# The order of 576 tasks, and the engine of 21 of them, in a fused attention and gated-MLP kernel on one core

## The chip, the core and the metric

The kernel runs on one core of one Trainium2 chip. Times are device microseconds (us) of one execution; the time of a kernel is the median of its runs. The core has five engines with a queue each: PE (matrix multiply), DVE (vector), ACT (activation functions), POOL (general, without access to PSUM) and SP, which only issues DMAs here. An engine works through its queue in program order and waits at an instruction until what it needs has been signalled.

## What is computed

A block with two branches over 2048 tokens of width 512. A vector `c` gives six modulation rows. Branch A is linear attention with 32 heads of 16 features, whose feature map is a pair of softmaxes; branch B is a gated MLP with 1376 hidden units. Inputs are bfloat16.

```
mod = silu(c) @ w_mod -> sa, ca, ga, sb, cb, gb
h = layernorm(x) * (1 + ca) + sa
q, k, v = split(h @ wqkv);  pq, pk = q @ w_phi, k @ w_phi        # per head
phi_q = [softmax(pq), softmax(-pq)];  phi_k = [softmax(pk), softmax(-pk)]
kv = sum over s of phi_k v;  z = sum over s of phi_k
o = (phi_q kv) / (phi_q z + 1e-6)
x = x + ga * (o @ wo)
h = layernorm(x) * (1 + cb) + sb
x = x + gb * ((sigmoid(h @ w_gate) * (h @ w_up)) @ w_down)
```

## The kernel before

The tokens are 16 tiles of 128. `w_phi` is folded into the weights of queries and keys, so one product gives `pk` directly. All work is cut into 1230 named tasks. Each task knows what it reads and writes and which engines may run it; one string, `ORDER`, lists all names, and that list alone decides the order. A name may carry the engine: `@A` for ACT, `@D` for DVE, `@P` for POOL; without it the first engine that the task allows is taken. `arrange` walks the list, checks that whatever a task needs stands ahead of it, and hands out buffers (8 PSUM banks, 7 feature buffers and so on) in the order in which the list sets them free; `emit` then issues the instructions:

```
for word in text.split():
    name, _, e = word.partition("@")
    t = self.tasks[name]
    t.eng = LETTER[e] if e else next(iter(t.alts))
    ...
    for b in t.bufs:
        if b.slot is None:
            b.slot = slots[b.cls].pop(0)
```

So each engine's queue is the list, cut down to the tasks of that engine. The lists of costs in the tasks are used by nothing in this program.

The names, by stage, with the lines of the profile (`t` is a tile, `g` a group of one or two tiles, `j` a quarter of the width):

- **Start.** `ld_*` are the loads on SP. `tpw` (PE) transposes the key weights, `wTc` (ACT, L664) copies them out of PSUM, `fold` (PE) multiplies them with `w_phi`, `foldc` (ACT, L685) copies the result. `st1_t` (DVE, L702/L703), `rs1_g`, `nmr1_g` and `xn1_t` (L727 on ACT, L731 on POOL) are the first normalization; `tph` (PE) or `xT1` (DMA) transposes it, `hm1_gj` (L751 on ACT, L753 on DVE or POOL) applies the modulation, which comes from `modc1` (PE) and `modc1c`.
- **Key pass**, for each tile: `K` and `V` (PE, L817 and L821), `e` (ACT, L776: two exponentials), `n` (DVE, L780: the sums), `r` (the reciprocal: L798 on DVE, L794 and L795 on ACT), `phi` (L787 on POOL or DVE), `va` (ACT, L836) and `kv` (PE, L282), which adds up in two PSUM banks for all 16 tiles. Features of tiles 11 and 13 to 15 go in four or two parts (`r14.4` is the part of tile 14 from group 4 on).
- **Hand-over.** `kvz0`, `kvn0`, `kvz1`, `kvn1` (DVE, L299 and L294) read the two banks when the last `kv` of each half is in.
- **Query pass**, for each tile: `Q`, `qe`, `qn`, `qphi` (L784), `pT` (a DMA that transposes), then `num` (PE, L326), `rd` and `u` (DVE), `oT`, `out` (PE, L356, with `wo` scaled by `ga` in `wo0` to `wo3` on POOL, L851), `x1`, `st2`, `rs2`, `xn2`. Queries of the first tiles run ahead, between the keys.
- **MLP**, in chunks of 1, 1, 2, 4, 4 and 4 tiles: `mod` (modulation), `gK.f` and `uK.f` (PE, L447: gate and up products of chunk K), `tg` (ACT), `hm` (DVE), `y` (PE, L485), `fin` and the store. `wd0` to `wd10` (POOL, L860) scale `w_down`.

The stages overlap as the list mixes them; nothing in the program waits for a whole stage.

Of the kernel before, what the change touches and what calls it, by code (L numbers as in the profile page):

```python
# [39 lines left out]
bd wdz warm0 c1 warm1_0 warm1_1 warm1_2 warm1_3 warm1_4 warm1_5 ld_x0b ld_x0a ld_wk0 tpw1 tpw0 warm1_6 warm1_7 c2 mask4 st1_3 st1_2 st1_1 ld_x1b rs1_2 rs1_1  # L40
nmr1_2 ld_wk1 xn1_3@A c3 wTc1 ld_x1a pmem tpw2 wTc0 nmr1_1 st1_6 wTc2 ld_wm00b st1_0 tpw3 xn1_1 tph13 tph10 xn1_2 tph22 tph20 tph21 wTc3 fold10 rs1_0@P fold12
st1_7 foldc10 ld_wm00a foldc12 fold11 modc1.0 rs1_4@P ld_x2b warm1_8 warm1_9 foldc11 modc1c0 st1_5 tph11 tph12 warm1_10 ld_wm01b warm1_11 st1_4 rs1_3@P
hm1_20@A xn1_0 nmr1_4 hm1_10 hm1_11@A hm1_21@A tph01 tph23 fold13 tph00 xn1_6 xn1_7 ld_wm01a st1_11 hm1_01@A foldc13 st1_10 modc1.1 K3a modc1c1@D ld_x2a
hm1_00@A tph02 nmr1_3 hm1_23 rs1_6@P hm1_13@A hm1_02 st1_9 st1_8 xn1_5 tph03 K0a tph41 hm1_03@A K2a tph40 xn1_4 hm1_22@A hm1_12@A hm1_41@A hm1_40 wqT1 nmr1_6
ld_x3a st1_15 fold01 K2b foldc01 tph42 hm1_42@A K0b K3b e0.0 ld_wv0 tph32 tph30 tph31 wqT3 tph33 rs1_5@P nmr1_5 K1a hm1_32 xn1_11 hm1_30@A st1_14 n0.0 st1_12
xn1_10 e2.0 xn1_9 K1b e3.0 rs1_8@P V3a V3b va3 V0a wqT2 xn1_8 V2a hm1_31@A V2b tph43 nmr1_8 xn1_15 xn1_14 ld_wmga wqT0 V0b fold03 V1a modca.0 modca.1 hm1_33
tph50 e1.0 n2.0 V1b K5a r0.0@A modcac hm1_50 n3.0 hm1_43@A foldc03 xT1_11 fold02 tph52 fold00 foldc02 phi0.0 va2 foldc00 xT1_10 va1 n1.0 va0 K5b K4a r3.0
st1_13 tph53 hm1_63@P hm1_60@P K4b hm1_62@P Q0 hm1_53@A tph51 Q1 ld_wmm2 r2.0@A tph82 hm1_51@A Q2 r1.0 phi3.0@D phi1.0@D qe0.0 Q4 hm1_82@A modc2.0 phi2.0@D
rs1_7@P nmr1_7 xn1_12 hm1_52 qe2.0 ld_wo xn1_13 kv0.0 kv1.0 kv2.0 tph83 kv3.0 qe1.0 qn0.0 qphi0.1@P xT1_12 e5.0 modc2.1 xT1_13 modc2c K6a K6b qphi0.0@P pT0
e4.0 qn2.0 tph80 qn1.0 hm1_80@A qphi2.1 qphi2.0 K7a K7b qe4.0 n4.0 V6 va6 r4.0@A n5.0 V5 va5 tph81 V4 qn4.0 phi4.0@D qphi1.1@P pT2 r5.0@A va4 qphi1.0@P  # L50
hm1_70@P K9 K8 hm1_61@P qphi4.0@P kv4.0 pT1 phi5.0 hm1_72@P qphi4.1 e6.0 hm1_83 hm1_81 V9 n6.0 V7 pT4 hm1_71 e9.0 va9 e7.0 va7 K11 n9.0 e8.0 e11.6 r6.0 r9.0@A
# [4 lines left out]
qn6.0 wo0 wo3 kv15.0 kvz0 kvn0 kv13.4 kv14.4 kv15.4 kvz1 kvn1 num0a num1a num2a wo2 rd0a wo_all rd1a qe3.0 u0a num0b num4a num1b rd0b Q11 qe5.0 rd2a u0b u2a
rd4a num2b qn3.0 u1a rd1b tpo0 Q8 qphi6.0@P qphi6.1@P oT0 out0 num4b rd2b u1b wd0 qe11.0 u2b qphi3.1@P qphi3.0@P x1_0 rd4b st2_0 qe8.0 Q7 qe7.0 tpo1 oT1 Q10
Q9 out1 Q15 oT2 rs2_0 qn5.0 nmr2_0 xn2_0 u4a u4b x1_1 qn7.0 tsw xnT0 out2 qphi5.1@P qphi5.0@P pT6 mod02 mod00 qphi7.0@P pT3 mod03@A mod01@A qe15.0 qphi7.1@P
Q13 g0.8 x1_2 tg0.8 g0.1 st2_1 wd1 rs2_1 tg0.1 u0.8 u0.1 g0.0 num3b g0.4 hm0.1 hm0.8 pT5 qe9.0 tg0.4 g0.9 wd2 u0.4 u0.9 rd3b u3b tg0.9 g0.5 num3a hm0.4 hm0.9
u0.2 u0.0 num6a tg0.5 tg0.0 rd3a u3a u0.5 g0.2 hm0.0 hm0.5 rd6a nmr2_1 qe10.0 tg0.2 oT4 g0.10 u0.10 wd6 hm0.2 g0.3 pT7 tg0.3 u6a g0.6 num6b u0.3 y0.0 y0.1  # L60
rd6b tg0.10 hm0.10 hm0.3 num5a num5b u6b rd5b wd3 wd4 wd5 oT3 oT6 xn2_1 qe13.0 tg0.6 rd5a y0.2 u5b g0.7 tg0.7 out4 u5a oT5 qn11.0 u0.6 u0.7 xnT1 num7a hm0.6
hm0.7 mod13@A mod12@A rd7a x1_4 y0.3 out3 qphi11.1@P qphi11.0@P x1_3 st2_3 out6 mod10@A mod11@A g1.2 tg1.2 g1.1 tg1.1 num7b wd7 u1.3 u1.2 hm1.2 u7a g1.4 u1.1
y0.4 rd7b hm1.1 u1.4 y0.5 tg1.4 hm1.4 g1.0 g1.10 u1.10 g1.3 u7b st2_2 rs2_2 tg1.10 tg1.3 hm1.10 hm1.3 pT11 out5 tg1.0 u1.7 g1.7 x1_6 nmr2_2 u1.0 hm1.0 g1.5
u1.5 x1_5 qn10.0 wd8 y0.6 g1.6 oT7 xn2_2 xn2_3 g1.8 y0.7 Q14 y0.8 wd10 tg1.7 tg1.5 hm1.5 out7 u1.8 u1.6 st2_4 tg1.6 xnT2 xnT3 wd9 x1_7 qphi10.0 Q12 hm1.7
st2_6 mod21@P mod20@P qphi10.1@P y1.0 pT10 tg1.8 mod22@A mod23@A hm1.6 g1.9 y1.1 y1.2 tg1.9 u1.9 y0.9 y1.3 y1.4 g2.5 y0.10 g2.6 st2_5 qe12.0 st2_7 hm1.8 qn9.0
tg2.5 qe14.0 rs2_4 hm1.9 rs2_3 nmr2_4 y1.5 u2.0 g2.1 g2.0 tg2.0 xn2_7@D hm2.0 nmr2_3 fin0 y1.6 g2.2 tg2.2 u2.6 u2.2 hm2.2 u2.1 num11b y1.7 g2.4 rd11b u11b
xn2_6@P xnT7 xnT6 u2.5 tg2.1 xn2_5 qphi9.1@P hm2.1 tg2.6 u2.8 xn2_4 hm2.5 g2.3 num11a rd11a u11a u2.9 qphi9.0@P xnT5 y1.8 xnT4 tg2.4 u2.4 hm2.4 hm2.6 tg2.3
g2.9 u2.3 hm2.3 g2.8 tg2.8 tg2.9 u2.7 mod41@P mod43@P mod32@P mod42@P mod31@P qn13.0 g2.10 hm2.8 g2.7 y1.9 num10a qn8.0 num10b y2.0 y1.10 tg2.7 hm2.7 rd10a
hm2.9 qphi8.0@P u2.10 pT9 y2.1 y2.2 y2.3 y2.4 y2.5 qn14.0 num9b rd9b qphi13.0 qphi8.1@P mod30@A mod33@A tg2.10 mod40@A y2.6 y2.7 g3.3 wr qphi13.1@P tg3.3 oT11
g3.0 u10a rd10b u10b pT8 oT10 hm2.10 qn15.0 g3.8 num9a rd9a u9a u3.0 out11 y2.8 g3.1 y2.9 qphi14.1 fin1 x1_11 u9b u3.3 hm3.3 st1 tg3.8 tg3.0 u3.8 num8a st2_11  # L70
num8b rd8b rd8a u8a pT13 qphi15.0 hm3.8 u8b u3.9 g3.4 u3.2 out10 x1_10 qphi14.0 oT8 oT9 hm3.0 st2_10 y2.10 g3.6 u3.6 qn12.0 rs2_6 out8 tg3.4 tg3.6 x1_8 hm3.6
# [987 lines left out]
```

## Time and profile before

| what | us |
|---|---|
| time before, median of 3 runs | 203.33 (203.19 to 203.52) |
| profiled execution, first to last instruction | 202.2 |
| DVE busy, whole span | 160.6 (79%) |
| ACT busy, whole span | 105.3 (52%) |
| POOL busy, whole span | 104.2 (52%) |
| first `num` of the query pass starts | 57.38 |
| first gate product of the second chunk starts | 77.5 |

The profiled execution has no time of its own beyond its span. The runs lie 1.0 to 1.3 us above that span, which is what lies around the first and the last instruction. The granted TensorE clock is 1.00 in every window up to 190 us and 0.97 behind it. All times within the execution are counted from its first instruction.

### The profile page before, as it was taken

The page shows a single profiled execution, that of the slowest core. Times are in us where ns is not written, and L with a number is a line of the kernel's source. Part 1 is how long each engine was busy: PE and PEld are TensorE (multiplying, and loading weights), DVE is VectorE, ACT ScalarE, POOL GpSimd, SP SyncE. Part 2 cuts the span into 40 slices and gives each one's busy share as a digit, 9 for nine tenths or more (in the row PEclk, how much of TensorE's full clock was granted, in tenths as well). Part 3 has the DMA queues.
Part 4 walks back from the last instruction along what each step waited for, and adds up shares of the span by engine and source line. Part 5 has one row for each costly group of instructions (what it writes and reads, how often), then busy time and mean ns, then how long its engine had stood idle before and what let it go on. Part 6 is the DMA issues. An engine that isn't in the chain of part 4 may idle for free.

```text
span 202.2 us, 4128 instructions
## 1 busy us (share of the span) xinstructions
PE 194.4 (96%) x1447; PEld 106.2 (53%) x1471; DVE 160.6 (79%) x376; ACT 105.3 (52%) x250; POOL 104.2 (52%) x146
## 2 busy tenths in 40 slices
...
DVE  3999999999999999998897796885969753326622
ACT  2899999999978975576531215212113420334100
POOL 3889978799699998867570066130030431000000
...
GB/s 169 329 262 239 289 232 111 114 71 261 396 254 77 133 109 51 82 39 108 117 79 80 53 79 85 100 104 52 26 26 81 2 78 54 28 5 26 28 54 57
DMA packets 49452, 22.92 MB, mean 113 GB/s; under 512 B 38065, under 2 KB 47634, under 8 KB 49426
## 3 DMA queue, kind: packets, MB, share of 16 engines
...
HBM read 11.58 MB, written 2.10 MB: 68 GB/s over the span
## 4 chain that ended last, share of the span: by engine, by line
PE 70%; ACT 15%; DVE 8%; issue 2%; POOL 2%; DMA 1%; POOLq 0%; DVEq 0%
PE y_ps L485 19%; PE u_ps L447 18%; PE g_ps L447 18%; PE a_ps L356 5%; ACT h1T L751 3%; ACT e L776 3%; ACT qe L776 2%; PE num L326 2%; PE k_ps L817 2%; DVE qks L780 2%; ACT wqk_f L685 2%; PE v_ps L821 2%; DVE ks L780 1%; DMA x_sb<-in_A_x_dram 1%; DVE phi L787 1%
## 5 line engine op out<-in xcount | busy, mean ns | idle before, releaser
L457 ACT ACTIVATE tg<-g_ps 128x512 bf16<-128x512 f32 (+5 forms) x66 | 28.7, 455 | 66.8 <-PE g_ps L447 39.9
L468 DVE SCALAR_TENSOR_TENSOR wmod_sb<-tg,u_ps 128x512 bf16<-128x512 bf16 (+4 forms) x63 | 30.2, 491 | 18.0 <-ACT tg L457 11.5
L485 PE MATMUL y_ps<-wd_sb,wmod_sb 128*128 128x512 bf16 (+4 forms) x180 | 44.2, 366 | 0.2
L447 PEld LDWEIGHTS <-wg_sb 128*128 128x128 bf16 (+1 forms) x252 | 21.9, 99 | 16.1 <-issue 0.2
L447 PEld LDWEIGHTS <-wu_sb 128*128 128x128 bf16 (+1 forms) x252 | 21.7, 99 | 15.9 <-issue 0.3
L784 POOL TENSOR_TENSOR qphi<-qe,qks 128x512 bf16<-128x512 bf16 x24 | 25.1, 1064 | 4.1 <-DMA pT<-qphi 1.4
L485 PEld LDWEIGHTS <-wmod_sb 128*128 128x128 bf16 (+1 forms) x187 | 17.1, 98 | 16.0 <-issue 0.6
L447 PE MATMUL u_ps<-wT_sb,wu_sb 128*128 128x512 bf16 (+2 forms) x124 | 23.8, 322 | 0.1
L447 PE MATMUL g_ps<-wT_sb,wg_sb 128*128 128x512 bf16 (+2 forms) x122 | 23.0, 321 | 0.2
L447 PE MATMUL g_ps<-wqk_sb,wg_sb 128*128 128x128 bf16 (+4 forms) x127 | 19.9, 287 | 0.1
L447 PE MATMUL u_ps<-wqk_sb,wu_sb 128*128 128x128 bf16 (+4 forms) x127 | 19.8, 286 | 0.2
L780 DVE TENSOR_REDUCE ks<-e 128x64 f32<-128x1024 bf16 (+2 forms) x22 | 19.3, 904 | 0.2
L492 DVE TENSOR_TENSOR ot<-y_ps,x 128x512 bf16<-128x512 f32 (+2 forms) x17 | 11.1, 654 | 10.1 <-PE y_ps L485 10.1
L780 DVE TENSOR_REDUCE qks<-qe 128x64 bf16<-128x1024 bf16 x16 | 19.1, 1204 | 0.0
L376 POOL TENSOR_SCALAR ve<-mv 128x2 f32<-128x2 f32 (+1 forms) x8 | 1.8, 226 | 33.4 <-DVE mv L366 33.3
L776 ACT ACTIVATE e<-k_ps 128x512 bf16<-128x512 f32 (+2 forms) x44 | 18.3, 536 | 0.0
L776 ACT ACTIVATE qe<-q_ps 128x512 bf16<-128x512 f32 x32 | 17.1, 612 | 0.8 <-POOL phi L787 0.6
L787 POOL TENSOR_TENSOR phi<-e,kr 128x1024 bf16<-128x1024 bf16 (+2 forms) x10 | 14.9, 1501 | 2.5 <-DVE phi L787 1.2
L817 PE MATMUL k_ps<-wqk_f,h1T 128*128 128x512 bf16 x61 | 16.1, 379 | 0.1
L356 PE MATMUL a_ps<-wo_sb,oT 128*128 128x512 bf16 x60 | 15.9, 379 | 0.2
L871 PE MATMUL q_ps<-wqk_f,h1T 128*128 128x512 bf16 x61 | 15.7, 379 | 0.2
L821 PE MATMUL v_ps<-wv_sb,h1T 128*128 128x512 bf16 x61 | 15.3, 379 | 0.1
...
## 6 DMA issues: line engine op xcount, KB each, us to landing
...
x_sb<-in_A_x_dram SPq DMA_DIRECT2D x6, 256.0 KB, 5.1
...
wd_sb<-in_B_w_down_dram SPq DMA_DIRECT2D x1, 1280.0 KB, 7.9
wmod_sb<-in_w_mod_dram SPq DMA_DIRECT2D x4, 256.0 KB, 6.2
wqk_sb<-in_A_wqkv_dram SPq DMA_DIRECT2D x2, 256.0 KB, 4.8
```

The source lines that it names most:

```text
L356: pe.matmul(ap_[:], lhsT=oT[:, j, :], rhs=wo_sb[:, j, :], start=(j == 0), stop=(j == KT - 1))
L447: pe.matmul(ps[:fsz, 0:n], lhsT=w[:, j, ft * P:ft * P + fsz], rhs=h[:, j, 0:n], start=(j == 0), stop=(j == KT - 1))
L457: G.add(f"tg{k}.{ft}", {"ACT": 0.13 + n * 0.00083}, lambda e, tg=tg, g_ps=g_ps, fsz=fsz, n=n: act.activation(tg[:fsz, 0:n], g_ps[:fsz, 0:n ...
L468: dve.scalar_tensor_tensor(hm_all[:fsz, hm[k].slot, ft, 0:n], tg[:fsz, 0:n], 1.0, u_ps[:fsz, 0:n], op0=ALU.add, op1=ALU.mult)
L485: mm = pe.matmul(y[:, 0:c1 - c0], lhsT=hm_all[:fsz, hm[k].slot, ft, tl * P:(tl + 1) * P], rhs=wd_sb[:fsz, ft, c0:c1], start=(ft == 0), sto ...
L776: act.activation(ee[:, a:b, s].rearrange("p g f h -> p g (f h)"), kp[:, a * 64:b * 64].rearrange("p (g n) -> p g n", n=64), ACT.Exp, scale ...
L780: dve.tensor_reduce(ks[:, a:b].rearrange("p g s h -> p (g s) h"), ee[:, a:b].rearrange("p g s f h -> p (g s) h f"), axis=AX.X, op=ALU.add)
L784: engine(e).tensor_tensor(ph[:].rearrange("p (g s f h) -> p g s f h", s=2, f=DH, h=4)[:, :, s], ee[:, :, s], ks[:, :, 1 - s].unsqueeze(2). ...
L787: engine(e).tensor_tensor(ph[:, a * P:b * P].rearrange("p (g f h) -> p g f h", f=DH, h=4), ee[:, a:b].rearrange("p g s f h -> p (g s) f h" ...
L817: pe.matmul(kp[:], lhsT=h1T[:, j, t * P:(t + 1) * P], rhs=wqk_f[:, j, D:2 * D], start=(j == 0), stop=(j == KT - 1))
L821: pe.matmul(vp[:], lhsT=h1T[:, j, t * P:(t + 1) * P], rhs=wv_sb[:, j, :], start=(j == 0), stop=(j == KT - 1))
L871: pe.matmul(qp[:], lhsT=h1T[:, j, t * P:(t + 1) * P], rhs=wqk_f[:, j, 0:D], start=(j == 0), stop=(j == KT - 1))
```

## The change

Only the string `ORDER` is replaced. The first 576 of its 1230 names, up to shortly ahead of the first gate product of the second chunk (`g1.2`), stand in another order; behind that the two lists are the same. The same tasks run. 21 of them run on another engine:

| tasks | from | to |
|---|---|---|
| `xn1_3` | ACT | POOL |
| `hm1_51` | ACT | DVE |
| `hm1_52`, `hm1_81`, `hm1_83` | DVE | ACT |
| `hm1_71` | ACT | POOL |
| `qphi0.0`, `qphi4.0` | POOL | DVE |
| `qphi2.0`, `qphi2.1` | DVE | POOL |
| `r8.0`, `r11.2` | DVE | ACT |
| `r14.4` | ACT | DVE |
| `phi8.0` | POOL | DVE |
| `phi11.0`, `phi11.2`, `phi11.4`, `phi13.0` | DVE | POOL |
| `mod00`, `mod02` | DVE | ACT |
| `mod03` | ACT | DVE |

One line of the string, before and after, shows its form:

```
-ld_wd2 n7.0 kv5.0 r7.0@A e11.2 gwa K14 e11.0 V8 e14.0 phi6.0 e14.4 e11.4 n8.0 n11.6 phi7.0@D n11.0 K10 n14.0 n11.2 r8.0 r11.0 kv6.0 hm1_73@P e10.0 gra va8 K12
...
+n11.6 e11.2 n11.2 r11.0 phi11.0 r11.6 r8.0@A phi8.0@D va8 e14.0 n14.0 va9 r14.4 r14.0 e10.0 n10.0 Q6 K12 e12.0 n12.0 kv8.0 kv9.0 r11.2@A e13.4 r10.0@A phi10.0@D
```

**ACT, the start** (from the third normalization task to the first modulations). Before, these rows stand in its queue:

```order
L710 ACTIVATE rs_84<-ve_83 128x1
L727 ACTIVATE xn<-x_sb,nmr,rs_84 128x512
L664 COPY wT_sb<-tp_w 128x4x128 x4
L685 CAST wqk_f<-fold_ps 128x512 x3
L635 COPY modc<-modc_ps 128x2
L636 ACTIVATE modc<-modc_ps 128x2
L751 ACTIVATE h1T<-tp_h,modc 128x256
```

And now these:

```order
L710 ACTIVATE rs_84<-ve_83 128x2
L664 COPY wT_sb<-tp_w 128x4x128 x2
L685 CAST wqk_f<-fold_ps 128x512
L664 COPY wT_sb<-tp_w 128x4x128 x2
L685 CAST wqk_f<-fold_ps 128x512 x3
L635 COPY modc<-modc_ps 128x2
L636 ACTIVATE modc<-modc_ps 128x2
L751 ACTIVATE h1T<-tp_h,modc 128x128
```

`xn1_3` (L727) is gone from the head of the queue, and all four `foldc` (L685) instead of three stand ahead of the modulation.

**POOL, the end of the key pass** (features `phi` of the keys, between them the scaling of `wo`). Before:

```order
L787 TENSOR_TENSOR phi<-e,kr 128x1024
L753 TENSOR_SCALAR h1T<-h1T,modc 128x256
L787 TENSOR_TENSOR phi<-e,kr 128x1024 x2
L787 TENSOR_TENSOR phi<-e,kr 128x256
L851 TENSOR_TENSOR wo_sb<-wo_sb,ga_sb 128x512
L787 TENSOR_TENSOR phi<-e,kr 128x512 x4
L851 TENSOR_TENSOR wo_sb<-wo_sb,ga_sb 128x512 x3
```

And now:

```order
L787 TENSOR_TENSOR phi<-e,kr 128x1024
L787 TENSOR_TENSOR phi<-e,kr 128x256
L851 TENSOR_TENSOR wo_sb<-wo_sb,ga_sb 128x512
L787 TENSOR_TENSOR phi<-e,kr 128x256 x3
L787 TENSOR_TENSOR phi<-e,kr 128x512 x5
L851 TENSOR_TENSOR wo_sb<-wo_sb,ga_sb 128x512 x3
```

The whole tile 8 (one of the 128x1024) is gone to DVE; three quarters of tile 11 and the first half of tile 13 have come, and `wo1` (the single L851) stands ahead of all but one of them.

**SP, the loads of the output weights.** Before, `ld_wo` (L557) is issued between the first transposes of normalized tiles; now it stands behind the load of `ga` (L846). Now:

```order
L692 DMA wd_sb<-in_B_w_down_dram 96x512
L843 DMA gdr_108<-gcol 128x4
L846 DMA ga_sb<-gdr_108 128x512
L557 DMA wo_sb<-in_A_wo_dram 128x4x512
L562 DMA wd_sb<-in_B_w_down_dram 128x10x512
L843 DMA gdr_109<-gcol 128x4
L561 DMA wu_sb<-in_B_w_up_dram 128x4x1376
```

In the list before, the same stretch reads:

```order
L692 DMA wd_sb<-in_B_w_down_dram 96x512
L843 DMA gdr_108<-gcol 128x4
L846 DMA ga_sb<-gdr_108 128x512
L843 DMA gdr_109<-gcol 128x4
L562 DMA wd_sb<-in_B_w_down_dram 128x10x512
L561 DMA wu_sb<-in_B_w_up_dram 128x4x1376
```

The load of `wo` has moved to just ahead of the load of `w_down`, and the write of `gb` (the second L843) one place back.

More of the change, by code (lines that the diff above doesn't have):

```diff
@@ L39 @@
 ORDER = """
[L40 to L51, printed above, removed]
@@ L52 @@
-ld_wd2 n7.0 kv5.0 r7.0@A e11.2 gwa K14 e11.0 V8 e14.0 phi6.0 e14.4 e11.4 n8.0 n11.6 phi7.0@D n11.0 K10 n14.0 n11.2 r8.0 r11.0 kv6.0 hm1_73@P e10.0 gra va8 K12
-phi9.0 kv7.0 K15 V13 n11.4 r11.2 V10 phi8.0 V11 n14.4 r14.0 r11.6 gwb e12.0 va10 K13 kv8.0 phi11.6 kv9.0 Q6 ld_wd r11.4 n10.0 r14.4@A wmod_free V14 phi11.4@D
-va11 n12.0 r10.0@A phi11.0@D phi11.2@D e13.4 phi10.0@D e13.0 e15.4 kv10.0 e15.0 kv11.4 kv11.6 ld_wu0 kv11.0 kv11.2 n13.4 va13 grb V12 Q3 wo1 phi14.0 r12.0@A
-phi14.4 V15 qe6.0 va12 n13.0 r13.4 phi13.4 n15.0 r13.0 n15.4 r15.4@A phi15.4 r15.0 va14 phi13.0@D phi15.0@D Q5 phi12.0@D ld_wg0 kv12.0 kv13.0 va15 kv14.0
@@ L56 @@
[L56 to L71, printed above, removed]
@@ new lines @@
+xn1_13 xT1_13 xn1_12 xT1_12 qn0.0 qphi0.1@P qn2.0 qphi2.1@P hm1_50 qphi0.0 pT0 qphi2.0@P pT2 e5.0 va7 hm1_51 qn1.0 K4b e4.0 n4.0 tph52 hm1_52@A Q4 qe4.0 K6a
+tph80 hm1_80@A n5.0 r4.0@A phi4.0@D V6 va6 qphi1.0@P qphi1.1@P qn4.0 qphi4.1 qphi4.0 pT1 pT4 tph82 K7b ld_wd2 gwa gra ld_wo ld_wd hm1_82@A modc2.0 modc2.1
+modc2c gwb ld_wu0 grb ld_wg0 r5.0@A K6b e6.0 n6.0 r6.0 tph83 K9 e9.0 n9.0 e7.0 n7.0 tph81 hm1_81@A hm1_83@A kv4.0 V8 K8 e8.0 n8.0 hm1_71@P hm1_62@P V10 va10
+r9.0@A K14 K11 e11.4 n11.4 phi5.0 kv5.0 V9 K10 hm1_72@P hm1_70@P phi6.0 hm1_73@P K13 r7.0@A phi7.0@D kv6.0 kv7.0 e11.0 e14.4 phi9.0 r11.4 n14.4 n11.0 e11.6
```

57 lines of the change are left out of this document (42 added, 15 removed).

## The prediction

> **What bounds the kernel now.** I began with the page: the totals, then the 40 slices.
>
> ```profile
> span 202.2 us, 4128 instructions
> PE 194.4 (96%) x1447; PEld 106.2 (53%) x1471; DVE 160.6 (79%) x376; ACT 105.3 (52%) x250; POOL 104.2 (52%) x146
> DVE  3999999999999999998897796885969753326622
> ACT  2899999999978975576531215212113420334100
> POOL 3889978799699998867570066130030431000000
> ```
>
> The totals mix stages. The slices (5.05 us each) show DVE full from slice 2 to 18, ACT full to slice 11, POOL close to full up to slice 14. So I asked for windows that end at the hand-over and at the second chunk. Behind each window stand its length, then busy time of PE, PEld, DVE, ACT and POOL.
>
> ```profile
> 7.30:56.00 48.70, 47.12 (x445) 26.37 (x450) 47.94 (x104) 47.87 (x128) 41.86 (x51) 1.00 0.93 226
> 57.40:77.50 20.10, 19.80 (x217) 13.21 (x221) 19.55 (x58) 16.87 (x41) 19.86 (x21) 1.00 0.68 114
> 77.50:202.20 124.70, 120.48 (x740) 63.32 (x752) 87.92 (x198) 36.70 (x74) 37.03 (x54) 1.00 0.30 59
> ```
>
> Through the key pass DVE (47.94 of 48.70) and ACT (47.87) are both full; POOL has 6.8 us free. Behind it PE is full: 19.80 of 20.10, then 120.48 of 124.70. Next came the chain of what ended last.
>
> ```profile
> 6.63 0.80 ACT xn L727
> 7.42 0.96 ACT wT_sb L664 x2
> 21.08 0.46 ACT h1T L751
> 31.12 0.97 ACT e L776 x2
> 35.65 1.22 DVE qks L780
> 55.69 1.13 DVE qks L780
> 57.38 0.93 PE num L326 x24
> 164.86 5.08 PE y_ps L485 x23
> ```
>
> It runs through ACT from 6.63 to 35, then mostly DVE to the hand-over, then PE. In the last row 23 products take 5.08 us, 0.22 each, without a gap. The products behind the first `num` are the same set in both orders, so **what the hand-over gains or loses reaches the end about one for one**; the rest of the list has little slack to give or take. The question is who is last at the hand-over (timeline rows, with what ended a wait):
>
> ```profile
> 54.49 0.25 ACT L794 ACTIVATE ks<-ks 128x32 f32<-128x32 f32 x1
> 54.97 1.06 ACT L836 CAST vaug<-v_ps 128x512 bf16<-128x512 f32 x2
> 51.42 3.06 POOL L787 TENSOR_TENSOR phi<-e,kr 128x512 bf16<-128x512 bf16 x3 [1.18 <-DVE phi L787]
> 55.14 1.46 POOL L787 TENSOR_TENSOR phi<-e,kr 128x512 bf16<-128x512 bf16 x1 [0.66 <-ACT kr L795]
> 55.62 1.21 DVE L780 TENSOR_REDUCE qks<-qe 128x64 bf16<-128x1024 bf16 x1
> 56.75 0.21 DVE L299 SCALAR_TENSOR_TENSOR kvb<-kvacc,mask 128x16 bf16<-128x16 f32 x1
> ```
>
> DVE takes `kvz0` at 56.75, the moment its last `qn` lets go. But ACT ends `va15` only at 56.03, and `kv15.0` needs that; POOL ends `phi15.4` at 56.60, and `kv15.4`, which stands ahead of `num` on PE, needs that. ACT is about 0.3 us and POOL about 0.2 us from being last.
>
> **The change, engine by engine, up to the hand-over.** Prices: mean durations of one.
>
> ```profile
> L787 DVE TENSOR_TENSOR phi<-e,kr 128x1024 bf16<-128x1024 bf16 x7 | 4.5, 673 | 0.0
> L787 DVE TENSOR_TENSOR phi<-e,kr 128x256 bf16<-128x256 bf16 x3 | 0.8, 295 | 0.0
> L787 DVE TENSOR_TENSOR phi<-e,kr 128x512 bf16<-128x512 bf16 x2 | 0.8, 432 | 0.0
> L753 DVE TENSOR_SCALAR h1T<-tp_h,modc 128x256 bf16<-128x256 bf16 x8 | 3.1, 401 | 0.0
> L798 DVE RECIPROCAL kr<-ks 128x64 bf16<-128x64 f32 x4 | 2.2, 538 | 0.0
> L787 POOL TENSOR_TENSOR phi<-e,kr 128x1024 bf16<-128x1024 bf16 x5 | 9.8, 1958 | 0.6 <-PE kvacc L282 0.3 <-ACT vaug L836 0.2
> L787 POOL TENSOR_TENSOR phi<-e,kr 128x256 bf16<-128x256 bf16 x1 | 0.6, 617 | 0.1
> L787 POOL TENSOR_TENSOR phi<-e,kr 128x512 bf16<-128x512 bf16 x4 | 4.5, 1152 | 1.8 <-DVE phi L787 1.2 <-ACT kr L795 0.7
> ```
>
> *DVE.* Two `hm1` go (2 x 0.40), `r8.0` (0.54), `r11.2` (a quarter; about 0.2), three quarters of a `phi` (3 x 0.30) and a half (0.43): 2.9 us. `phi8.0` (0.67) and `r14.4` (about 0.3) come: 1.0. `hm1_51` against `hm1_52` and two `qphi` against two cancel. Neighbours on DVE overlap by some 0.08 us, and six fewer instructions give back 0.5, so DVE is **1.3 to 1.4 us shorter**; alone it would bring `num` from 57.4 to 56.1.
>
> *ACT.* `hm1_81`, `hm1_83`, `r8.0` and `r11.2` come; `hm1_71` and `r14.4` go. An `hm1` costs 0.46 (the chain row at 21.08); an `r` takes from 54.49 to 54.97, 0.48, with a whole one nearer 0.55. So 2 x 0.46 + 1.05 - 0.46 - 0.55 = **+0.9 us**, on a queue with no room. `xn1_3` (0.80) also leaves, but it lay in front of `wTc`, where ACT now waits for the transposes of the key weights:
>
> ```profile
> 6.47 0.72 PEld L661 LDWEIGHTS <-wqk_sb 128*128 128x128 bf16 x8 [0.52 <-DMA wqk_sb<-in_A_wqkv_dram]
> ```
>
> The weights land at 6.47, and their load keeps its place on SP. `wTc0` needs the second of two transposes, so ACT begins at about 7.2 to 7.35, against 7.33 before: what goes there buys 0 to 0.1 us. The short waits that ACT has now can go (48.70 - 47.87, 0.8 us at most). Some go for certain, since a fourth `foldc` covers the wait for the modulation; others stay, as the next `hm1` still waits for the second half of the weights of the modulation. I take 0.3. So `va15` ends at 56.03 + 0.9 - 0.3 = 56.6, with ends at 56.1 and 57.0. From `va15` to `num` took 57.38 - 56.03 = 1.35, of which some 0.3 was DVE's `qn`; **`num` then starts at 57.6, between 57.1 and 58.0**. The reduction of DVE is waited away: its last sums (`n10`, `n15`) need `e` from an ACT that is later, and `qn` needs nothing new. The cover that DVE had is gone; late next is ACT.
>
> *POOL.* `phi8.0` (1.96) goes; `xn1_3` (0.8), `hm1_71` (0.6), three quarters (3 x 0.62) and a half (1.05 to 1.15) come; `qphi` cancels. That is +2.3 us, beside 6.8 us free, but the last half stands right ahead of `phi15.4`. On PE `num` stands behind `kv15.4`: with `r13.0` out on DVE at 53 to 54.2, two halves of 1.05 give 55.1 to 56.3 for POOL's end: no bound, if nothing stops them. Price at the hand-over: 0 here, up to 0.9 in the third rival.
>
> *SP.* The load of `wo` moves behind that of `ga`.
>
> ```profile
> 38.87 1.23 SPq L874 DMA_TRANSPOSE pT<-qphi  x1
> 43.29 0.33 SPq L846 DMA_DIRECT2D ga_sb<-gdr  x1
> ga_sb<-gdr SPq DMA_DIRECT2D x1, 256.0 KB, 4.9
> wd_sb<-in_B_w_down_dram SPq DMA_DIRECT2D x1, 1280.0 KB, 7.9
> 49.02 1.22 POOL L851 TENSOR_TENSOR wo_sb<-wo_sb,ga_sb 128x512 bf16<-128x512 bf16 x1
> ```
>
> `ga` lands 4.9 us behind its issue, at 48.2, or some 0.8 earlier if the `pT` ahead of it (38.87) is. 512 KB of `wo` come behind it. The 1280 KB of `w_down` were in 7.9 us from issue at 44.16, at 52.1, so 3.9 us behind `ga`; two fifths of that is 1.5. I put `wo` at 48.6 to 49.7. `wo1` now stands ahead of three quarters of tile 11 and five halves: from 48.6, 1.1 + 3 x 0.57 + 5 x 1.05 = 8.1 us give 56.7, just POOL's end of before. So the stall costs nothing at its early end and 1.1 us at its late one; I take 0.1.
>
> *Behind the hand-over.* Two of `mod0` go to ACT, one comes back. In 57.40 to 77.50 PE has 0.3 us free, the most that a better order can regain; I take 0.1.
>
> Sum: `num` at 57.6 against 57.4, +0.2; +0.1 for POOL; -0.1 behind: 202.2 + 0.2 = 202.4 for the span. The runs lie 1.1 us above it (203.33 is the median of the runs shown), so **203.5 us**; its own range is 203.0 to 203.8.
>
> **Two rules of the Trainium skill.** POOL's last `phi` took 1.46 us; the three ahead of it took 3.06, 1.02 each. The long one ran beside a `phi` of DVE. The Trainium skill, "SBUF — State Buffer", section "Who interferes with whom", says that VectorE and GpSimd hold one shared port pair for a whole instruction, so that one blocks the other; a product of two SBUF operands counts. The row agrees. By that rule the two halves of POOL and the two last `phi` of DVE cannot overlap, which is the third rival. The second rule: "Perfetto Trace Analysis", section "Identifying the Most-Contended Engine", of the same skill has headroom of TensorE judged by weight loads; 53% would leave room, the first rival would hold to the end, and the time would be 202.0. But the 23 products of 0.22 us above leave no gap, and a load takes under half of that, so I don't follow it.
>
> **The rivals.**
>
> 1. *DVE alone is the bound.* ACT regains all its waits and POOL is never late: 203.3 - 1.3 = **202.0 us**. For it: DVE is last in the chain at 55.69. Against: ACT's margin is 0.3 us and it gets 0.9 more.
> 2. *Half of it holds.* `num` comes when ACT's early end allows, at 57.1, and PE's 0.3 us behind it are regained: **202.8 us**.
> 3. *POOL becomes last: slower.* Behind `r13.0` (53 to 54.2) come on one port two halves on POOL (2 x 1.05) and two `phi` on DVE (0.6 + 0.35): 3.05 us, to 57.25, where it was 2.35 before and ended at 56.60; or `wo` lands at 49.7. Then `kv15.4` and with it `num` and `kvn1` come 0.6 to 1.1 later: **204.2 us**. It decides from the point at which `phi15.4` ends later than 56.9. For it: 1.46; the stalls of POOL on DVE's `phi` in the price rows (1.2). Against: POOL's 6.8 us of room.
>
> That the program doesn't do what the list says can be left out: the queues show it.
>
> **Chances.** Forecast 0.42, first rival 0.10, second 0.16, third 0.32. The range of 8 in 10 takes in the second rival and the third up to 1.1 us: 202.6 to 204.4. Runs differ by 0.16%, so about 0.2% (0.4 us) can be told from no change. Faster by more: 0.26 (the first two rivals); within: 0.42; slower by more: 0.32.
>
> **What would show it.** ACT: `wTc` starts at 7.2 to 7.35, no wait on ACT from there on, `va15` ends at 56.3 to 56.9. DVE: waits for ACT's `e` (L780 behind L776) of 1 us or more in all between 45 and 57, where there are none now. POOL: `wo1` waits for a DMA; `phi15.4` ends at 56.3 to 57.0. PE: `num` starts at 57.3 to 57.9, and from there to the second chunk's first gate product 20 us again. I am wrong if DVE still has no wait and `num` starts below 57; if ACT starts `wTc` before 7.1; or if the time moves behind 77.5.

## The result, and the profile after

The changed kernel takes **208.82 us** (median of 6 runs, 208.16 to 210.63), the kernel before 203.43 (203.19 to 204.33, 6 runs): a ratio of 1.0269, with a 95% interval of 1.0234 to 1.0304. It is slower by 2.7%, where 203.5 was forecast with a range to 204.4. The profiled execution of the changed kernel took 209.78 us, a long one of the six, so its rows stand some 1 us above the median. In the executions with both figures on record the time lies 1.7 to 2.1 us above the span, not 1.0 to 1.3; so the profiled execution of the kernel before, with its span of 202.2, took about 203.9 us, some 0.5 above its own median. Ratios, here and below, are to the kernel before on the same chip and leave out executions that were disturbed as a whole (one of a_slot took 230.3 us), while medians take all in.

The page, its span and the 40 slices (5.2 us each) of the three engines that the prediction watched:

```profile
span 208.0 us, 4149 instructions
DVE  3999989999899978999798799594969844326631
ACT  2899999799967967456651224142113320334100
POOL 4999989855999997867681036340030332000000
```

DVE and ACT now have gaps ahead of slice 12, and POOL is full around the hand-over. Windows cut at the same places in the program (first `num` at 61.30, first `g1.2` at 82.9; behind each stand its length and the busy time of PE, PEld, DVE, ACT, POOL):

```profile
7.30:56.00 48.70, 45.21 (x429) 25.20 (x429) 46.91 (x95) 46.01 (x124) 42.23 (x53) 1.00 0.85 207
56.00:61.30 5.30, 4.13 (x45) 2.21 (x44) 4.88 (x10) 4.29 (x10) 5.30 (x5) 1.00 0.91 294
61.30:82.90 21.60, 20.45 (x221) 13.40 (x221) 19.43 (x58) 16.36 (x39) 19.91 (x21) 1.00 0.54 104
82.90:208.00 125.10, 121.14 (x754) 63.37 (x752) 87.88 (x198) 36.71 (x74) 37.04 (x54) 1.00 0.30 59
```

`num` comes at 61.3 instead of 57.4 (+3.9); from there to `g1.2` it takes 21.6 instead of 20.1 us (+1.5); behind that 125.1 instead of 124.7. So the time is lost in two stretches, and the 5.8 us of the span are there: 3.9 + 1.5 + 0.4. Neither DVE nor ACT is full to 56 us (46.9 and 46.0 of 48.7): no engine "is the bound" any more. Three places in the trace show what the engines wait for. Three links of the chain of what ended last (start, length):

```profile
38.24 2.15 DVE qphi L784
57.27 1.25 DVE phi L787
58.54 1.15 DVE phi L787
```

One row of the DMA issues between 40 and 56 us (the last number is the time from issue to landing):

```profile
wo_sb<-in_A_wo_dram SPq DMA_DIRECT2D x1, 512.0 KB, 6.5
```

And timeline rows (start, length of all the merged instructions, and in brackets the idle time before and what ended it):

```profile
38.07 2.03 POOL L787 TENSOR_TENSOR phi<-e,kr 128x1024 bf16<-128x1024 bf16 x1 [0.37 <-ACT e L776]
40.41 1.09 ACT L776 ACTIVATE e<-k_ps 128x512 bf16<-128x512 f32 x2 [1.52 <-DVE qphi L784]
41.55 1.74 PE L817 MATMUL k_ps<-wqk_f,h1T 128*128 128x512 bf16 x6 [1.03 <-ACT e L776]
...
51.49 1.16 POOL L851 TENSOR_TENSOR wo_sb<-wo_sb,ga_sb 128x512 bf16<-128x512 bf16 x1 [2.13 <-DMA wo_sb<-in_A_wo_dram]
52.61 8.00 POOL L787 TENSOR_TENSOR phi<-e,kr 128x256 bf16<-128x256 bf16 x8
57.25 2.44 DVE L787 TENSOR_TENSOR phi<-e,kr 128x1024 bf16<-128x1024 bf16 x2
61.29 0.84 PE L326 MATMUL num<-kvb,pT 128*128 128x68 bf16 x20 [0.33 <-DVE kvb L294]
...
76.60 1.08 ACT L776 ACTIVATE qe<-q_ps 128x512 bf16<-128x512 f32 x2 [1.48 <-POOL wd_sb L860]
77.74 0.45 PE L326 MATMUL num<-kvb,pT 128*128 128x68 bf16 x8 [1.13 <-ACT qe L776]
```

For comparison, from the kernel before: the mean of such a half on DVE (the group between 8 and 57 us; 420 ns), and DVE's last three `phi`:

```profile
L784 DVE TENSOR_TENSOR qphi<-qe,qks 128x512 bf16<-128x512 bf16 x3 | 1.2, 420 | 0.0
54.31 1.39 DVE L787 TENSOR_TENSOR phi<-e,kr 128x512 bf16<-128x512 bf16 x3
```

- **At 38 us.** `qphi4.0`, now on DVE, takes 2.15 us, where such a half takes 0.42. It starts while POOL is in `phi5.0` (38.07 to 40.10) and ends 0.3 us behind it, as if it ran when POOL was done. `e7.0` on ACT takes the feature buffer that `qphi4.0` gives back, and waits 1.52 us; PE waits 1.03 us behind that.
- **At 49 to 61 us.** `wo` lands 6.5 us behind its issue at 44.87, at 51.4. `wo1` waits 2.13 us for it, and the eight products behind it take 8.00 us, to 60.6. DVE's last two `phi` (0.68 and 0.41 in the kernel before) take 2.44, since they run in turn with POOL's.
- **At 75 us.** `qe10.0` waits 1.48 us, and `num5b` on PE stands behind it. The row names a scaling on POOL; the experiments show another cause.

### The profile page after: what moved, and what is told of

Same layout as the page of the kernel before. It is cut to its first block, busy times and chain, and to the rows that moved or that the text cites. A ratio compares the mean times of both kernels' runs of the same rounds, so it can differ in the third digit from the quotient of the medians.

```text
span 208.0 us, 4149 instructions
## 1 busy us (share of the span) xinstructions
PE 197.0 (95%) x1471; PEld 106.4 (51%) x1471; DVE 163.2 (78%) x369; ACT 106.3 (51%) x253; POOL 108.5 (52%) x151
## 4 chain that ended last, share of the span: by engine, by line
PE 63%; ACT 13%; DVE 10%; POOL 7%; DMA 3%; issue 2%; SPq 0%; POOLq 0%; ACTq 0%; DVEq 0%
PE y_ps L485 19%; PE g_ps L447 16%; PE u_ps L447 16%; PE a_ps L356 5%; ACT e L776 3%; POOL xn L731 3%; ACT qe L776 2%; DVE phi L787 2%; PE k_ps L817 2%; DVE qks L780 2%; DMA pT<-qphi 2%; DMA x_sb<-in_A_x_dram 1%; PE num L326 1%; ACT h1T L751 1%; PE g_ps L449 1%
## 5 line engine op out<-in xcount | busy, mean ns | idle before, releaser
L485 PE MATMUL y_ps<-wd_sb,wmod_sb 128*128 128x512 bf16 (+4 forms) x187 | 45.7, 367 | 0.0
L447 PE MATMUL g_ps<-wqk_sb,wg_sb 128*128 128x256 bf16 (+4 forms) x128 | 20.0, 287 | 0.0
L492 DVE TENSOR_TENSOR ot<-y_ps,x 128x512 bf16<-128x512 f32 (+2 forms) x17 | 11.1, 654 | 10.1 <-PE y_ps L485 10.1
L787 POOL TENSOR_TENSOR phi<-e,kr 128x512 bf16<-128x512 bf16 (+2 forms) x13 | 16.7, 1304 | 3.1 <-DVE phi L787 1.7
L821 PE MATMUL v_ps<-wv_sb,h1T 128*128 128x512 bf16 x64 | 15.9, 379 | 0.0
```

Of the source, the lines that this page charges most:

```text
L447: pe.matmul(ps[:fsz, 0:n], lhsT=w[:, j, ft * P:ft * P + fsz], rhs=h[:, j, 0:n], start=(j == 0), stop=(j == KT - 1))
L485: mm = pe.matmul(y[:, 0:c1 - c0], lhsT=hm_all[:fsz, hm[k].slot, ft, tl * P:(tl + 1) * P], rhs=wd_sb[:fsz, ft, c0:c1], start=(ft == 0), sto ...
L787: engine(e).tensor_tensor(ph[:, a * P:b * P].rearrange("p (g f h) -> p g f h", f=DH, h=4), ee[:, a:b].rearrange("p g s f h -> p (g s) f h" ...
L821: pe.matmul(vp[:], lhsT=h1T[:, j, t * P:(t + 1) * P], rhs=wv_sb[:, j, :], start=(j == 0), stop=(j == KT - 1))
```

## The experiments

Two measures are worked out from each trace, so that kernels with other orders can be compared. **Lost time**: the start of a product of PE less the durations of all products ahead of it (0.216 us for 512 columns, others as their rows run back to back); its growth in a stage is what PE lost there. **Stretched**: what DVE's rows up to 62 us took above the quick quarter of rows of the same operation and shape in all traces, where that is more than 0.1 us. The stages end after the same amount of PE's work: at 10 us of it (about 20 us on the clock), 30 us (about 41), the first `num`, and `g1.2`. Each row is one profiled execution.

| kernel | median us | lost at start | first half of key pass | to `num` | to `g1.2` | DVE stretched |
|---|---|---|---|---|---|---|
| before | 203.4 | 10.4 | 0.6 | 1.0 | 0.5 | 0.0 |
| changed | 208.8 | 9.7 | 2.3 | 3.9 | 1.9 | 3.8 |
| a_wo_early | 208.9 | 10.1 | 2.2 | 2.3 | 2.3 | 2.9 |
| a_wo1_late | 208.7 | 11.7 | 0.6 | 2.2 | 2.9 | 1.4 |
| a_q4_pool | 208.8 | 10.2 | 0.7 | 4.0 | 2.0 | 2.6 |
| a_three | 209.2 | 9.7 | 1.4 | 3.1 | 2.9 | 2.7 |
| b_q4_dve | 206.1 | 10.0 | 1.8 | 2.4 | 0.5 | 2.5 |
| b_wo_late | 207.7 | 9.9 | 0.6 | 4.1 | 2.3 | 2.4 |
| a_eng_before | 213.5 | 10.9 | 3.8 | 5.5 | 1.5 | 1.3 |
| b_eng_after | 211.3 | 11.0 | 0.7 | 6.5 | 2.1 | 4.3 |
| a_slot | 207.2 | 9.7 | 0.7 | 3.6 | 0.5 | 1.9 |
| b_qn6 | 204.9 | 10.1 | 0.6 | 2.3 | 1.6 | 1.5 |
| a_slot_wo | 207.2 | 9.8 | 2.4 | 2.7 | 0.6 | 3.6 |
| a_p13 | 210.3 | 9.8 | 2.4 | 3.8 | 1.4 | 3.3 |
| h_ab | 207.4 | 10.2 | 2.2 | 1.4 | 0.5 | 0.0 |
| h_ba | 206.3 | 10.7 | 0.6 | 2.8 | 0.6 | 1.5 |
| a_fix3 | 206.7 | 10.0 | 1.2 | 2.8 | 0.7 | 2.6 |
| a_fix4 | 207.1 | 10.0 | 1.4 | 2.2 | 1.0 | 1.7 |
| a_fix5 | 207.7 | 9.7 | 1.1 | 3.1 | 0.9 | 1.6 |

Names with a_ start from the changed kernel, with b_ from the one before. The start varies by some 0.5 us between executions of the same start. The 11.7 of a_wo1_late is the clock: the granted TensorE clock was 0.50 from 13.8 to 17.2 us in that execution. Stalls vary too (below): the table shows where time goes, the medians what it comes to. The stretched rows of DVE are not the whole loss: a_eng_before has 1.3 us of them at 213.5 us, and h_ab none at 207.4.

**The suspects, each undone in the changed kernel.**

```diff
 a_wo_early:  ld_wmm2 +ld_wo ...  gra -ld_wo ld_wd
 a_wo1_late:  V14 -wo1 kv10.0 ...  rd0b u0a +wo1 wo2 wo3 wo0
 a_q4_pool:   qphi4.1 -qphi4.0 +qphi4.0@P pT1 pT4
 a_three:     all three
```

> The changed kernel, with the load of wo issued early again (behind the last of the first weight loads, where the kernel before has it); nothing else. Theory L (the late wo holds up POOL, and POOL is last at the hand-over): wo1 starts at about 49.4 instead of 51.5, the eight last phi of POOL end near 58.0 to 58.6 instead of 60.6, num starts near 58.5 to 59.3 instead of 61.3, and the time is 208.8 - 2.0 to 2.8 = 206.0 to 206.8 us. Theory A (ACT or DVE would be last anyway, the wait of POOL is cover for them): within 0.4 us of 208.8.

> The changed kernel, with wo1 moved behind phi15.4, so that no scaling of wo stands among the features; the load of wo stays late. Theory L: the wait of 2.1 us and the 1.16 us of work both leave POOL's way to the hand-over, phi15.4 ends near 57.3 (bounded by r13.0 of DVE), num starts near 58.0, and the time is near 208.8 - 3.2 = 205.6 us (205.0 to 206.3); about 1 us less than with the early load. If only the wait counts and the work lies beside something else, both kernels come out alike. Theory A: within 0.4 us of 208.8.

> The changed kernel, with qphi4.0 back on POOL; nothing else. Theory P (DVE and POOL shut each other out in such products: qphi4.0 on DVE waited for the whole of phi5.0 on POOL, took 2.14 us, and e7.0 on ACT waited 1.52 us for its buffer): e7.0 starts 1.2 to 1.5 us earlier, DVE has no row of 2 us there, pT4 and the load of wo behind it come about 1 us earlier too, and the time is 208.8 - 0.8 to 1.6 = 207.2 to 208.0 us, though POOL gets 1.06 us more work. Theory W (the stall is only the work that DVE got, 0.43 us, and POOL is short of time): slower, 208.8 + 0.3 to 1.1 us.

> The changed kernel with all three edits: wo loaded early, wo1 behind phi15.4, qphi4.0 on POOL. If the three account for the loss: num starts near 57.0 instead of 61.3, the wait of qe10.0 near 75 shrinks as pT5 comes earlier, and the time is within 0.8 us of the kernel before, 202.7 to 204.2 us. If ACT's 0.9 us more work then bounds the hand-over, as was forecast: va15 ends at 56.5 or later with no wait on ACT, and the time is 203.5 or more. If something else makes up the loss (the new order as such): over 205 us.

Measured: 208.94 us (1.0261 [1.0226, 1.0296]), 208.70 (1.0239 [1.0192, 1.0285]), 208.80 (1.0265 [1.0240, 1.0290]) and 209.16 (1.0300 [1.0255, 1.0345]). No edit moved the median by more than 0.4 us, so the gains that were expected of the suspects all failed to come; what came true on the time is the other outcome named for a_wo_early, a_wo1_late (within 0.4 us of 208.8) and a_three (over 205, something else makes up the loss). In its own stage each edit did something: the early `wo` brings "to `num`" from 3.9 to 2.3, `qphi4.0` on POOL the first half from 2.3 to 0.7. But the gain did not reach the end. With `qphi4.0` on POOL the next product of DVE, `phi7.0`, takes 1.54 us behind POOL's `phi6.0`; with `wo` early, `wo1` still waits, 0.45 us for `ga`; with `wo1` late, `out0` on PE waits 0.9 us for POOL's scaling instead. So none of them explains the loss alone, and two were tried in the order of before, where nothing else is changed.

**The same two in the kernel before.**

```diff
 b_q4_dve:   -qphi4.0@P +qphi4.0@D
 b_wo_late:  ld_wmm2 ... -ld_wo ...  gra +ld_wo
```

> The kernel before, with one name changed: qphi4.0 runs on DVE instead of POOL. Theory P (such a product of DVE waits until POOL's instruction has ended, and the other way round): POOL, free earlier, starts phi5.0 at 37.3 to 37.5 instead of 38.80, DVE's qphi4.0 and qphi4.1 wait behind it until about 39.4 (one row of over 2 us), the saturated DVE and then the hand-over come 1.3 to 2.2 us later, and the time is 204.6 to 205.6 us. Theory W (only work counts): DVE gets 0.43 us more, POOL 1.06 us less, and the time is 203.4 to 203.9 us.

> The kernel before, with the load of wo moved from 21.5 to right behind the load of ga, as in the changed kernel; nothing else. If a late load of wo costs the loss by itself: wo lands 49.5 to 51, wo1 waits 0.5 to 2 us, and the time is 1 to 2 us above 203.4. If it costs only because in the changed kernel eight features stand behind wo1 with no gap: POOL's gaps of before (1.18 and 0.66 us, behind wo1) take the wait up, and the time is within 0.4 us of 203.4.

Measured: b_q4_dve 206.10 us, 1.0148 [1.0089, 1.0207], a little above the range of the theory of exclusion (P) and far above that of work alone (W). Timeline rows of b_q4_dve:

```profile
36.84 2.00 POOL L787 TENSOR_TENSOR phi<-e,kr 128x1024 bf16<-128x1024 bf16 x1 [0.63 <-PE k_ps L817]
37.10 2.35 DVE L784 TENSOR_TENSOR qphi<-qe,qks 128x512 bf16<-128x512 bf16 x2
```

Two halves of 0.42 take 2.35 us, because POOL, relieved of `qphi4.0`, began its own product 0.26 us ahead of them. Taking 1.06 us of work off POOL and giving 0.42 to DVE made the kernel 2.5 us slower. Sums of work can't give that; in the trace what changed is who comes first. It is the clearest single test, though not of one meeting alone: `phi12.0` at 56.4 us is stretched too, by 0.85 us.

b_wo_late: 207.72 us, ratio 1.0126 [1.0053, 1.0199]. Its quickest execution took 205.29 us; two of the four, the profiled one among them, had a mean granted clock of 0.983 and took 208.3 and 208.4. The hope that POOL's gaps would take the wait up failed. Its timeline:

```profile
50.48 1.38 POOL L851 TENSOR_TENSOR wo_sb<-wo_sb,ga_sb 128x512 bf16<-128x512 bf16 x1 [1.93 <-DMA wo_sb<-in_A_wo_dram]
51.83 4.24 POOL L787 TENSOR_TENSOR phi<-e,kr 128x512 bf16<-128x512 bf16 x4
54.18 3.74 DVE L787 TENSOR_TENSOR phi<-e,kr 128x512 bf16<-128x512 bf16 x3
57.97 2.00 PE L282 MATMUL kvacc<-vaug,phi 128*128 128x68 bf16 x32 [2.80 <-DVE phi L787]
```

POOL did catch up: its last `phi` ends at 56.1, ahead of the 56.6 of before. But it had no gap left, and DVE's last three `phi` took 3.74 us between POOL's instead of 1.4 (0.45, 0.41 and 0.68, with some overlap). PE stood still for 2.80 us. In this execution the path from the late DMA to the end runs through the exclusion, not through POOL's own length, and the clock adds to it (last section).

**Order alone, engines alone.**

```diff
 a_eng_before:  the new order, all 21 engines as before
 b_eng_after:   the old order, all 21 engines as changed
```

> The changed kernel's order, with all 21 engines as before. If the 21 engines are the cause: within 1 us of the kernel before, 202.7 to 204.5 us. If the order is the cause by itself (late wo, buffers that come free later, products of DVE beside POOL's): 206 us or more, with wo1 still waiting for its DMA and num5b still waiting behind qe10.0.

> The order of the kernel before, with the 21 engines of the changed kernel. Theory P (products of DVE and instructions of POOL shut each other out): qphi4.0 alone has cost 2.5 us in that order; with four more phi on POOL, the last ones end later than 57.5 and DVE's stretched rows sum to 2 us or more (there are none in the kernel before): 206 to 209 us. Theory W (only the sums of work count: DVE 1.3 us less, POOL 2.3 us more, of 6.8 us free): 202.5 to 204.0 us.

Measured: 213.54 us (1.0501 [1.0451, 1.0550]) and 211.32 (1.0362 [1.0323, 1.0401]). Both halves of the change are worse alone than together (1.027): order and engines fit each other, and the loss can't be divided between them. a_eng_before is in the range of the second outcome, but `wo1` waits for no DMA there, and with 1.3 us of stretched rows most of its 10 us is not explained. b_eng_after came out above its range; DVE's stretched rows sum to 4.3 us there.

**The wait at 75 us, and a try to speed up the hand-over of before.**

```diff
 a_slot:  qphi5.0@P -pT5 Q13 ... qphi7.0@P qphi7.1@P +pT5 pT7
 b_qn6:   kv14.0 -qn6.0 wo0 ... u0b +qn6.0 u2a
```

> The changed kernel with the name pT5 moved behind qphi7.1 in the list: every queue keeps its instructions in their order, but qe10.0 now gets the feature buffer that qphi7.1 sets free instead of the one that pT5 sets free. If the wait of 1.48 us on ACT ahead of qe10.0 at 75 us, and of 1.1 us on PE ahead of num5b behind it, is that buffer: qe10.0 starts 1 us or more earlier, the lag of PE no longer grows at num5b, and the time is 208.8 - 1.0 to 1.4 = 207.4 to 207.8 us. If something else holds qe10.0 or num5b there: within 0.4 us of 208.8.

> The kernel before, with the sum qn6.0 on DVE moved from ahead of kvz0 to behind u0b. If the hand-over is passed on to the end one for one: kvz0 starts near 56.4 instead of 56.75 (then bounded by ACT's va15 and POOL's phi15.4), num near 57.0 instead of 57.4, and the time is 0.2 to 0.4 us below the kernel before. If the products of the query pass take the gain back, as u2a and u1a come 1.2 us later: no change, or up to 0.3 us slower.

a_slot: 207.20 us, 1.0165 [1.0119, 1.0212], 1.6 below the changed kernel and 0.2 below the range expected. No queue differs in the order of its instructions; only buffers do. Timeline rows of a_slot:

```profile
37.30 0.76 DVE L784 TENSOR_TENSOR qphi<-qe,qks 128x512 bf16<-128x512 bf16 x2
37.85 1.98 POOL L787 TENSOR_TENSOR phi<-e,kr 128x1024 bf16<-128x1024 bf16 x1 [0.76 <-ACT e L776]
...
74.50 0.42 PE L326 MATMUL num<-kvb,pT 128*128 128x68 bf16 x8
```

The wait of 1.13 us ahead of `num5b` (last row) is gone, and the loss to `g1.2` is 0.5 as before: shown. In the changed kernel `qe10.0` had been given the buffer that the DMA `pT5` sets free, which landed at 76.25; POOL's scaling, which the row named, was not it. The first two rows are the place at 38 us, untouched by this edit: in this execution DVE was ready first, by 0.55 us, and its two halves took 0.76 instead of 2.48. The DMA `pT0`, on which it waits, had landed 0.6 us earlier. So the same instructions lose 1.7 us there or nothing, by who comes first. The executions of the changed kernel scatter by 2.5 us and those of before by 1.1; such meetings may be a reason, but that is not shown, as one execution of each is kept.

b_qn6: 204.89 us (12 runs, 204.26 to 206.15), 1.0055 [1.0030, 1.0079]: 1.1 us slower by the ratio, where at most 0.3 was allowed for. In its profiled execution `phi12.0` on DVE started 0.1 us behind POOL's `phi15.4` and took 1.53 us; in the kernel before it started 0.12 ahead and took 0.68.

**Halves of the new order, and more single edits.**

```diff
 a_slot_wo:  a_slot and a_wo_early
 a_p13:      a_slot_wo, and ... kv12.0 -phi13.0 +phi13.0@D kv13.0
 h_ab:       the new list up to kv4.0 (wo early, other early loads as before), then the old one
 h_ba:       the old list up to V9, then the new one with a_slot
```

> The changed kernel with two edits: the buffer edit of the run before (pT5 named behind qphi7.1) and the load of wo early, as in the kernel before. Theory P+L (the late wo makes POOL late, and POOL and DVE then shut each other out at the end of the key pass): wo1 starts near 47.5 to 48.5 instead of 49.5, phi15.4 ends 1 us or more earlier, and the time is 205.4 to 206.6 us, 0.6 to 1.8 below the buffer edit alone. If the end of the key pass takes it all back: 207.2 us again.

> As the run beside it, and phi13.0 on DVE again. Theory P: POOL's last stretch loses a product that took 1.50 us beside a product of DVE, DVE gets one of 0.45; phi15.4 ends 1 us or more earlier, and the time is 0.5 to 1.2 us below the run beside it (204.4 to 205.8). Rival 1 of the prediction (DVE is the bound, and more work on it costs): 0.4 us above the run beside it.

> The order and engines of the changed kernel up to the first kv of tile 4 (about 38 us), with the early load of wo and without its other early loads, and from there on the order and engines of the kernel before. If the first part of the new order costs nothing: 202.8 to 204.2 us. If it is faster, as PE's lag at 15 us (9.8 against 10.7) hints: 202.5 to 203.0. If it carries part of the loss: 205 or more.

> The order and engines of the kernel before up to V9 (about 38 us; wo loaded early, qphi4.0 on POOL), and from there on those of the changed kernel, with the buffer edit. If the second part of the new order carries the loss by itself: 205.0 to 207.0 us, with DVE's stretched rows summing to 1.5 us or more. If the loss needs the late wo or the first part: within 0.6 us of the kernel before, 202.9 to 204.2 us.

Measured: a_slot_wo 207.24 us (1.0161 [1.0105, 1.0217]), no gain over a_slot, as in the second outcome. Its stage "to `num`" is 0.9 better, but the stall at 38 us was there again (2.12 us), and `ga` came late behind it. a_p13 210.25 (1.0287 [1.0192, 1.0381]): slower than the run beside it, but a bad test, since `phi13.0` stands behind `qn6.0` in DVE's queue and PE waited 2.3 us for it. h_ab 207.43 (1.0178 [1.0121, 1.0234]) and h_ba 206.34 (1.0115 [1.0059, 1.0171]): each half of the new order carries a loss by itself, of 3.9 and 2.8 us by the medians. h_ba came out as expected, with 1.5 us of stretched rows. h_ab's time is in the third outcome, but it has no stretched row of DVE (in its quickest execution, 206.08, which is the profiled one), and it loses 2.2 us in the first half of the key pass, where the kernel before loses 0.6. POOL's rows are the longer ones there (`hm1` at 26.4 takes 1.58 instead of 0.56), and `phi5.0` comes 1.4 us later than in the kernel before. Two rows of h_ab show what it waits for:

```profile
40.17 1.91 POOL L787 TENSOR_TENSOR phi<-e,kr 128x1024 bf16<-128x1024 bf16 x1 [1.73 <-DMA pT<-qphi]
42.14 0.43 PE L282 MATMUL kvacc<-vaug,phi 128*128 128x68 bf16 x8 [0.88 <-POOL phi L787]
```

POOL stood still for 1.73 us until a transposing DMA had landed, and PE 0.88 us behind that `phi`. What makes this DMA late in h_ab was not tried.

**Three fixes together, and a test of why they don't add up.**

```diff
 a_fix3:  a_wo_early, a_q4_pool and a_slot
 a_fix4:  a_fix3, and r15.0 +phi13.0@D phi12.0@D ... kv12.0 -phi13.0 kv13.0
 a_fix5:  a_fix4, and qphi4.1 +hm1_71@P +hm1_62@P qphi4.0@P
```

> The changed kernel with three edits, one for each stage: wo loaded early, qphi4.0 on POOL, and the buffer edit (pT5 named behind qphi7.1). If the losses of the stages add up, as the single edits showed them (first stage 0.7 instead of 2.3, hand-over 2.3 to 2.7 instead of 3.9, behind it 0.5 instead of 1.9): 1.4 to 1.8 us above the kernel before, 204.8 to 205.4 us. If a stall that is removed only comes back in the next stage, as with the single edits of wo and of qphi4.0: 206.5 us or more.

> As the run beside it, and phi13.0 on DVE again, right behind r15.0 (ahead of phi12.0), so that POOL has one product less next to DVE's last three. Theory P: POOL's phi15.4 ends 0.8 to 1.5 us earlier, num comes 0.5 to 1.2 us earlier, and the time is 0.4 to 1.2 us below the run beside it. If DVE's products only wait in another place (three instead of two behind POOL's): no change, or slower.

> As the run before with four edits (a_fix4), and hm1_71 and hm1_62 moved ahead of qphi4.0 in POOL's queue, where POOL waited 2.5 us for DVE's qn4.0. Nothing else. In a_fix4 phi7.0 on DVE stood 1.0 us behind phi6.0 on POOL (1.68 us instead of 0.68), e14.4 on ACT waited 0.87 us for its buffer behind it, and PE lost 1.0 us at K13. Theory P: phi6.0 now ends 1.1 us earlier, ahead of phi7.0's start; that row is back at 0.7 us, the wait of e14.4 and the step at K13 are gone, and the time is 0.7 to 1.1 us below a_fix4 and a_fix3: 205.6 to 206.2 us. If POOL's work as such were short there (not its place beside DVE): no change, 206.6 to 207.1.

Measured: a_fix3 206.67 us (1.0166 [1.0147, 1.0186]), a_fix4 207.06 (1.0201 [1.0155, 1.0247]), a_fix5 207.72 (1.0212 [1.0177, 1.0247]). None gets below 206.5: a_fix3 and a_fix4 are in the outcome in which a stall that is removed only comes back, and a_fix5 is above both of its ranges. Timeline rows of a_fix3:

```profile
43.41 1.91 POOL L787 TENSOR_TENSOR phi<-e,kr 128x1024 bf16<-128x1024 bf16 x1
44.18 1.68 DVE L787 TENSOR_TENSOR phi<-e,kr 128x1024 bf16<-128x1024 bf16 x1
45.35 0.83 ACT L776 ACTIVATE e<-k_ps 128x256 bf16<-128x256 f32 x3 [0.86 <-POOL phi L787]
```

And of a_fix5:

```profile
42.09 1.91 POOL L787 TENSOR_TENSOR phi<-e,kr 128x1024 bf16<-128x1024 bf16 x1
43.95 0.69 DVE L787 TENSOR_TENSOR phi<-e,kr 128x1024 bf16<-128x1024 bf16 x1
49.18 1.16 POOL L851 TENSOR_TENSOR wo_sb<-wo_sb,ga_sb 128x512 bf16<-128x512 bf16 x1 [1.21 <-DMA ga_sb<-gdr]
54.95 2.77 DVE L787 TENSOR_TENSOR phi<-e,kr 128x512 bf16<-128x512 bf16 x3
```

In a_fix3 the stall of 38 us is back at 44 us: `phi7.0` takes 1.68 us behind POOL's `phi6.0`, and `e14.4` waits for the buffer. a_fix5 moves two instructions of POOL into its idle time ahead, and as the theory says the row is at 0.69 and the wait of ACT gone. The time didn't follow: DVE came 1.0 us earlier to its last products than in a_fix4, but POOL waited 1.21 us for `ga`, which no edit had moved, and ran beside DVE again; three products of DVE took 2.77 us, where the kernel before takes 1.4. At each place the rows go as the exclusion says; that one fix makes the kernel quicker is not borne out.

## Why the prediction was wrong

- **The step that failed** is the one on POOL: "Price at the hand-over: 0 here", because 6.8 us of POOL were free. And ahead of it the rule that a product moved costs its duration from the price rows: 0.42 for a half on DVE. Shown in its place: such a product of DVE and an instruction of POOL don't run at once, so what is left of the other engine's instruction adds to the price when that comes first (2.15 us for 0.42). The kernel before has no row on DVE stretched by more than 0.1 us up to the hand-over: in its list POOL is idle, nearly done or just behind at each `phi` of DVE, and where the two meet POOL waits (1.46 us at 55.14). How much of the 5.4 us is the exclusion's can't be told, as the single edits don't add up; 1.6 us are the buffer of `qe10.0` (below). I read those gaps of POOL as room (51.42 with "1.18 <-DVE phi" stood in the fence) and not as what kept DVE quick.
- **The third rival was the right mechanism and too small.** It was given 0.32, only at the last products, with 0.6 to 1.1 us as its price, through POOL's end. It was there at four places on DVE (26.6, 38, 52 and 57 to 60 us; 3.8 us in all). POOL's rows, measured in the same way, were stretched by 4.2 us, against 1.6 in the kernel before and 3.6 in h_ab; the profile's lengths on POOL are rough. `num` came 3.9 us later, not 0.2.
- **`wo` at 48.6 to 49.7** was mis-sized: it landed at 51.35. Its issue was 1.2 us later than assumed, since `pT4` ahead of `ga` on SP waits for `qphi4.0`, which stood behind POOL; and it took 6.5 us from issue to landing. The sum from `wo1` to `phi15.4`, 8.1 us, came out as 9.1, as products stretched. A late `wo` alone costs 1.7 us in the quickest execution of b_wo_late, and 2.6 by its ratio.
- **ACT as the next bound** never came to the test: ACT had waits of 1.52 us ahead of 40.4 and 0.29 at 52.9; `va15` ended at 58.3, later than the 56.3 to 56.9 forecast, and was still not last, as POOL ended at 60.6. DVE waited 0.9 us between 50 and 57, but for POOL (the two waits are ahead of reciprocals and end with a `phi` of POOL, which gives back their buffer), not for ACT's `e` as forecast.
- **"-0.1 behind"** was +1.4 in lost time: a step that the prediction did not have. Moving a name moves the buffer that a later task is given (`qe10.0` behind `pT5`). Shown by a_slot.
- **Right:** what the hand-over loses reaches the end one for one (b_q4_dve: 2.2 us more lost time than before at `num`, and 2.2 at `g1.2` and at the last product; the spans differ by 1.8); `wo1` waits for a DMA; nothing moves behind 77.5 that isn't late before. DVE's list is shorter, as worked out (163.2 us busy less 3.8 stretched, against 160.6), and it did not matter. `wTc` began at 6.69, ahead of the 7.1 that the prediction named as a sign of being wrong: the transposes ahead of it began at 5.96 instead of 6.47, when their DMA had landed. PE had lost 0.7 us less at 20 us; that was no gain in the end.
- **The sum's 1.1 us** from span to time should have been 1.7 or more, as the result section has it. With 1.7 the sum is 204.1 us, against some 203.9 for the execution that it starts from; the forecast difference of 0.2 us stays.

What stays open: how the 5.4 us divide between the exclusion, the late `wo` and waits of the kind that h_ab shows; what makes a_eng_before the slowest; and whether any list with these 21 engines can beat the kernel before; none of the runs did.
